# Z's scratch by pairs of classes: two pieces of 90 rows a block, spread over the partitions

## The chip, the cores and the metric

The kernel runs on one NeuronCore of one Trainium2 chip. The metric is the device time of one execution in microseconds; lower is better. PE is the matrix engine (TensorE), DVE the vector engine, ACT the scalar engine, POOL is GpSimd and SP the sync engine. SP and POOL issue all DMAs of this kernel, SP on one queue and POOL on another, and both queues are served by the same 16 DMA engines.

## The reference

The input x has 8 sequences of 5,696 steps with 128 channels; h is one filter of the same length and width. The first half is a causal convolution of x with h by FFTs of double length, the second half a mixing of the lowest 64 frequencies, followed by a dense layer with a ReLU.

```python
def _attn_ref(x, h):
    L = 2 * S
    Xf = np.fft.rfft(x, n=L, axis=1)
    Hf = np.fft.rfft(h, n=L, axis=0)
    return np.fft.irfft(Xf * Hf[None, :, :], n=L, axis=1)[:, :S, :]

def _moe_ref(x, w_r, w_i, w_ch):          # x is the result above
    X = np.fft.rfft(x, axis=1)
    Yr = einsum('bmd,mde->bme', Xr, w_r) - einsum('bmd,mde->bme', Xi, w_i)   # the first 64 modes
    Yi = einsum('bmd,mde->bme', Xr, w_i) + einsum('bmd,mde->bme', Xi, w_r)
    u = x + np.fft.irfft(Y, n=S, axis=1)
    return u + np.maximum(u @ w_ch, 0.0)
```

## The kernel before

A step of the sequence is written as J q + p with J = 64 and q below NQ = 89. The DFT of double length is split into a transform over q, which gives NK = 90 classes, and one over p. The batch is worked in four pairs of sequences (`g_` 0 to 3), and each pair in NT = 23 ticks of KT = 4 classes (the last has two).

In a tick PE forms the spectra of the tick's classes (matmuls of As with M), DVE multiplies them with the filter's (U from Xs and Hs), PE transforms back over p (U with Wc), and ACT writes the result, Z, to a tile of SBUF. A tile of Z has 128 partitions, the real and imaginary part (`ri`) of 64 positions p, and in its free dimension the class, the sequence of the pair and the 128 channels. Z then goes to a scratch in DRAM, `zscr`, one write of 256 KB per tick, issued by SP. PE also uses the Z tile on the spot for the 64 modes (matmuls with G, the accumulator XT).

The output part needs Z the other way round, with the 90 classes and two parts as the contraction. So it reads `zscr` back in 16 blocks, four per pair, each with 16 positions p: 180 rows (class, part) of 8 KB. A block has a room of two tiles, ZTa with rows 0 to 127 and ZTb with rows 128 to 179 in partitions 32 to 83, where partitions 0 to 31 are zero. There are NC = 5 rooms (ZT0 to ZT4), which lie over buffers of the forward part that are dead by then. For each position PE multiplies ZTa with the table S4a (128 rows) and ZTb with S4b (84 rows), into the same accumulator; the term of the 64 modes comes on top (table IB with C). ACT and DVE copy the result to UT, PE multiplies it with the identity and w_ch together (WI), ACT takes the ReLU (R), DVE adds (O), and SP writes the output.

The order is the program's: each operation is recorded with what it reads and writes, and each engine runs its own operations in that order, waiting on semaphores. In the last pair `early` hangs loads for the output part on ticks, all issued by POOL: the identity at tick 0, four parts of the mode weights W at ticks 1, 3, 6 and 8, the table S4b at tick 12, S4a at 16, and at tick 21 blocks 0, 1 and 2 with IB between. Each of those up to tick 16 waits for its tick's U (`pace`). After the last pair POOL issues WI and blocks 3 and 4. Block 0 waits in addition for the Z writes of the last pair's ticks 0 to 14 (`SLACK`). Blocks 5 to 15 are issued by SP, each when the room of the block five ahead of it has been used up, in one queue with the output's writes.

Before it loads a room for the first time, `load_zt` clears partitions 0 to 31 of ZTb with a memset on POOL (L477); the load of that tile follows on the same engine.

While PE waits for the modes' result, it does the Z part of four tiles of block 0 ahead (`u_z(..., alone=True)`); the rest of the work on a tile is in `u_tile`.

Of the kernel before, what the change touches and what calls it, by code (L numbers as in the profile page):

```python
# [4 lines left out]
P = 128  # L5
F16 = mybir.dt.float16
F32 = mybir.dt.float32
U32 = mybir.dt.uint32
# [115 lines left out]
def bass_long_conv_fft__then__afno_spectral_mix_kernel(nc, x, h, moe_w_r, moe_w_i, moe_w_ch, out):  # L124
    B, S, D = x.shape
    M = moe_w_r.shape[0]
    assert D == P and M == 64 and B == 8
    J = 64
    NQ = S // J
# [26 lines left out]
    pos = J * qq[None, :] + pp[:, None]  # L156
    ang = 2.0 * np.pi * kk[:, None, None] * pos[None] / L
    s4 = np.stack([back[:, None, None] * np.cos(ang), -back[:, None, None] * np.sin(ang)], axis=0)
    RB, PB = 2 * NK - P, 32
    rows = s4.transpose(1, 0, 2, 3).reshape(2 * NK, S)  # L160
    s4t = np.zeros((P, 2 * S))
    s4t[:, 0:S] = rows[0:P]
    s4t[PB:PB + RB, S:2 * S] = rows[P:2 * NK]
    tt = np.arange(S)
    am = 2.0 * np.pi * np.outer(tt, np.arange(M)) / S
    modes = np.concatenate([np.cos(am), -np.sin(am)], axis=1)
# [75 lines left out]
    xt = at("XT", B * XTW, F16, a_g + GW * 2 + 2048 * (NZX - NZ))  # L242
    assert GW * 2 + 2048 * (NZX - NZ) + B * XTW * 2 <= HW * 2

    ZB = 16
    NC = 5
    ZP = ZB * 2 * D
# [33 lines left out]
    def pv(bank, off, dims, p0=0, n=P):  # L281
        return bass.AP(ps, p0 * 4096 + bank * 512 + off, [[4096, n]] + [list(d) for d in dims])

    R = Recorder(nc)
    for name, n in (("c", 16), ("x", 26), ("z", 8), ("w", 16), ("t", 10), ("s", 8), ("o", 12), ("p", 16), ("q", 10)):
        R.ring(name, n)

    def bank(i):
        return ("bank", i)
# [18 lines left out]
    def dma(eng, dst, src, ring, reads=(), writes=(), after=()):  # L308
        R.add(eng, lambda h_: h_.dma_start(dst, src), reads, writes, ring=ring, after=after)  # L309

    def mm(o, l, r, st, sp, reads, writes):
        R.add("tensor", lambda h_: h_.matmul(o, l, r, start=st, stop=sp), reads, writes)  # L312
# [3 lines left out]
    def once(key, toks):  # L316
        if key in first:
            return []
        first[key] = 1
        return list(toks)  # L320
# [145 lines left out]
    ZX = [("zs", i, b) for i in range(NZ, NZL) for b in range(2)]  # L466
    zt_old = [(H_ALL, H_ALL), (AST, AST), (H_ALL, H_ALL), (AST, AST), (M_ALL[3:6], G_ALL)]

    def load_zt(i, eng="sync", more=()):
        g_, c_ = divmod(i, J // ZB)  # L470
        for part, (p0, r0, n) in enumerate(((0, 0, P), (PB, P, RB))):
            old = once(("zt", i % NC, part), zt_old[i % NC][part])
            if more:
                old = list(old) + list(more)
            if old and part:
                z32 = zt[i][1][0:PB, :].bitcast(U32)
                R.add("gpsimd", lambda e: e.memset(z32, 0), (), [("zt0", i)], after=old)  # L477
            dma(eng, bass.AP(zt[i % NC][part], p0 * ZP, [[ZP, n], [1, ZP]]),
                bass.AP(zs, (g_ * 2 * NK + r0) * J * 256 + c_ * ZB * 256, [[J * 256, n], [1, ZP]]),
                "q" if eng == "gpsimd" else "t", [("zd", g_, s_) for s_ in range(NT)], [("zt", i % NC, part)], after=old)  # L480

    def load_ib():
        dma("gpsimd", ib_sb[:, :], c_ib.ap(), "p", (), [("ib",)], after=M_ALL[0:2] + pace)

    def load_s4(part):
        n = PB + RB if part else P
        dma("gpsimd", s4_sb[part][0:n, :], bass.AP(c_s4, part * S, [[2 * S, n], [1, S]]), "p", (),
            [("s4", part)], after=pace + (AST if part else M_ALL[1:4]))

    V, A = "vector", "scalar"  # L490
    border = {NT - 1: [(0, 2, V)], NT: [(1, 0, V), (2, 2, A)], NT + 1: [(3, 0, V), (4, 2, A)], NT + 2: [(5, 0, V), (6, 2, V)]}
    early = {0: lambda: load_id(), 1: lambda: load_w(0), 3: lambda: load_w(1), 6: lambda: load_w(2), 8: lambda: load_w(3),
             12: lambda: load_s4(1), 16: lambda: load_s4(0),
             NT - 2: lambda: (load_zt(0, "gpsimd", SLACK), load_ib(), load_zt(1, "gpsimd"), load_zt(2, "gpsimd"))}
    pace = []
    SLACK = [("zd", NP - 1, s_) for s_ in range(NT - NZL)]
# [4 lines left out]
    def load_wi():  # L501
        dma("gpsimd", wi_sb[:, P:2 * P], bass.AP(c_w, 2 * P, [[3 * P, P], [1, P]]), "p", (), [("i16",)], after=M_ALL[5:6])
        dma("gpsimd", wi_sb[:, 0:P], moe_w_ch, "w", (), [("wch",)], after=M_ALL[5:6])
# [33 lines left out]
    def tick(g_, t):  # L537
        if g_ + 1 < NP:
            for i in range(2 * XC):
                if t == XPLACE[g_ > 0][i]:  # L540
                    x_place(i, x_st[i], xtok(i))
        with_h = with_h_at(g_, t)
        if t < NT:
            sl = XSLOT[0] if with_h else XSLOT[(t + (g_ == 0)) % 2]
            for i, k in enumerate(ticks[t]):
                for r in range(2):
                    for b in range(2):
                        col = k * 3 * J + (J if r == 0 else 0) + b * J
                        mm(pv(sl + b, i * D, [[1, D]]),
                           ap(m_sb, MW, J * b, J, col, [[1, P]]),  # L550
                           ap(a_sb, AW, J * b, J, (2 * k + r) * D, [[1, D]]), r == 0, r == 1,
                           AST + mtok(k), [bank(sl + b)])
            products(g_, t, sl)
        if t in border and g_ + 1 < NP:
            for j, sl, e in border[t]:
                a_tile(j, [sl], e)
        if g_ + 1 < NP and t % 2 == 0 and 0 < t <= 4 * XC:
            i = t // 2 - 1
            x_load(g_ + 1, i, x_st[i], xtok(i), [("u", t % NU)] + AST)
        if LC <= t < NT + LC:  # L560
            s_ = t - LC
            n = len(ticks[s_])
            i, zi = s_ % NU, s_ % NZS[g_]
            zb = [turns("z", ZBANK) for b in range(2)]
            for b in range(2):
                for r in range(2):
                    mm(pv(zb[b], 0, [[1, n * D]]), (W1, W2)[r], u_s[i][:, r * 1024 + b * 512:r * 1024 + b * 512 + n * D],
                       r == 0, r == 1, [("u", i), ("wc",)], [bank(zb[b])])
                evac(bass.AP(z_s[zi], b * D, [[1024, P], [2 * D, n], [1, D]]),
                     pv(zb[b], 0, [[D, n], [1, D]]), [bank(zb[b])], [("zs", zi, b)], eng="scalar",  # L570
                     after=once(("zx", zi, b), Z_OLD) if zi >= NZ else ())
            zo = (g_ * NK + KT * s_) * P * 256
            dma("sync", bass.AP(zs, zo, [[256, P], [P * 256, n], [1, 256]]),
                bass.AP(z_s[zi], 0, [[1024, P], [256, n], [1, 256]]), "z",
                [("zs", zi, 0), ("zs", zi, 1)], [("zd", g_, s_)])
        if LM <= t < NT + LM:
            s_ = t - LM
            zi = s_ % NZS[g_]
            if s_ == 0:
                mm(pv(MB, 0, [[1, 2 * P]]), m_sb[ZR:P, 0:P], ap(f1_sb, 2 * NK, ZR, P - ZR, 0, [[0, 2], [1, P]]), True, False, [("f1",)] + mtok(0), [bank(MB)])  # L580
            for i, k in enumerate(ticks[s_]):
                for b in range(2):
                    if k % 2:
                        o, off, n, sl = pv(MB, b * P, [[1, P]]), (k + 1) // 2 * P, P, (k + 1) // 2
                    else:
                        ms, off = even[k]
                        n, sl = 2 * len(ms), 0
                        dims = [[M, 2]] if len(ms) == 1 else [[ms[1] - ms[0], 2], [M, 2]]
                        o = pv(MB, b * P + ms[0], dims)
                    mm(o, z_s[zi][:, i * 256 + b * P:i * 256 + b * P + P], g_sb[:, off:off + n],  # L590
                       False, k == NK - 1 and b == 1, [("g", sl // GP), ("zs", zi, b)], [bank(MB)])
        if with_h:
            filter_tick(t + LH, [2, 3])
# [26 lines left out]
                    dma("gpsimd", dst, src_, ring, (), [tok], after=[("as", j)])  # L620


    load_wi()
    load_zt(3, "gpsimd")
    load_zt(4, "gpsimd")

    LSLOT = [4, 6, 0, 2]
# [4 lines left out]
    def u_z(i, b, half, alone=False):  # L632
        g_, c_ = divmod(i, NCH)
        t = turns("l", LSLOT)
        z = zt[i % NC]
        for hb in range(2):
            if alone:
                mm(pv(t + hb, 0, [[1, 4 * NQ]]), f1_sb[ZR:P, 0:P], ap(f1_sb, 2 * NK, ZR, P - ZR, 0, [[0, 2], [1, 2 * NQ]]),
                   True, False, [("f1",)], [bank(t + hb)])
            else:  # L640
                u_c(i, b, half, t, hb, True)
            for pl in range(4):
                for ri in range(2):
                    pz = half * 8 + hb * 4 + pl
                    so = (c_ * ZB + pz) * NQ
                    n = (P, PB + RB)[ri]
                    mm(pv(t + hb, pl * NQ, [[1, NQ]]), z[ri][0:n, pz * 256 + b * P:pz * 256 + b * P + P], s4_sb[ri][0:n, so:so + NQ],
                       False, not alone and pl == 3 and ri == 1, [("zt", i % NC, ri), ("zt0", i % NC), ("s4", ri)], [bank(t + hb)])
        if alone:
            ahead[(i, b, half)] = t  # L650
        return t
# [149 lines left out]
```

## Time and profile before

Three runs took 405.23, 405.71 and 408.66 us; the median is 405.71. The profiled execution took 409.74 us, of which the profiled span is 407.7 us.

| engine | busy us | share of the span | instructions |
|---|---|---|---|
| PE (matmul) | 376.7 | 92% | 5398 |
| PEld (weight load) | 286.7 | 70% | 5398 |
| DVE | 311.8 | 76% | 341 |
| ACT | 296.4 | 73% | 477 |
| POOL | 81.4 | 20% | 133 |

Over the span the 16 DMA engines moved 105.8 MB, 260 GB/s in the mean, in 86,720 packets. The mean granted clock of PE was 0.977. The four pairs of the forward part end near 272 us, and the output part fills the rest.

The shares are means over stages with different limits, so the windows and the waits say more than this table. A row of the groups gives the line, the engine, what is written from what, the count, the busy time and the mean of one in ns, and the idle time ahead of it with what ended it. Lines 300 to 309 and 312 are helpers (`evac`, `dma`, `mm`), so operations are told apart by their tiles. In this profile ZT0a and ZT0b are the two tiles of a room.

### The profile page before, as it was taken

To read this page: it belongs to the slowest core of one execution; us is meant where nothing else is said; L and a number is where in the kernel's file an instruction comes from. 1 tells how busy PE (TensorE), PEld (TensorE's weight loads), DVE (VectorE), ACT (ScalarE), POOL (GpSimd) and SP (SyncE) were. 2 spreads that over 40 slices of the span, in tenths; PEclk is the share of its full clock that TensorE was granted. 3 is DMA by queue.
4 is the path that set the end of the run, shared out by engine and by line. 5 is a ranking of instruction groups with operands and counts; after the bars stand their busy time and mean duration, and the time that the engine had idled before them with its cause. 6 is when DMAs were issued, how large, how long until landed. Compare 5 with 4: busy or idle time off the path is not lost.

```text
span 407.7 us, 12527 instructions
## 1 busy us (share of the span) xinstructions
PE 376.7 (92%) x5398; PEld 286.7 (70%) x5398; DVE 311.8 (76%) x341; ACT 296.4 (73%) x477; POOL 81.4 (20%) x133
## 2 busy tenths in 40 slices
PE   7979899998999988899989899997978999999994
PEld 7978666656756657656658666665767889888873
DVE  6878789997899997889997888850324677777876
ACT  1458599987978977788878888960434777777775
POOL 8300022210823202723304011039100000000000
PEclk9999999999999999999999999995798999999999
DMA  8997379995989993989985499999998999999869
GB/s 159 194 320 271 101 162 280 274 278 159 138 137 218 251 233 80 141 154 207 245 224 95 48 311 346 285 274 394 417 390 340 314 350 420 406 419 390 347 251 357
DMA packets 86720, 105.81 MB, mean 260 GB/s; under 512 B 22494, under 2 KB 72286, under 8 KB 82846
## 3 DMA queue, kind: packets, MB, share of 16 engines
q1 hardware_dynamic: 62379, 67.73, 48.1%
q0 software_dynamic: 24288, 37.31, 43.0%
q8 instruction: 42, 0.69, 0.7%
q14 instruction: 11, 0.09, 0.1%
HBM read 72.49 MB, written 51.12 MB: 303 GB/s over the span
## 4 chain that ended last, share of the span: by engine, by line
PE 56%; DMA 14%; DVE 11%; ACT 9%; POOL 6%; issue 2%; SPq 0%; DVEq 0%; POOLq 0%
PE ps L312 56%; DVE U L528 5%; DMA ZT4b<-zscr 5%; DVE As L306 5%; DMA Xr<-in_x_dram 4%; ACT As L302 4%; DMA zscr<-Zt 3%; POOL Xr L309 2%; DMA Hs<-Hs 2%; ACT Xs L300 2%; ACT R L735 1%; ACT UT L300 1%; ACT Zt L300 1%; DVE Xin L348 1%; POOL ZT1b L477 0%
## 5 line engine op out<-in xcount | busy, mean ns | idle before, releaser
L528 DVE TENSOR_TENSOR U<-Xs,Hs 128x2048 f16<-128x2048 f16 x70 | 82.7, 1190 | 20.2 <-ACT Xs L300 20.0
L312 PE MATMUL ps<-U,Wc 128*128 128x512 f16 (+1 forms) x368 | 93.6, 377 | 1.9 <-DVE U L528 1.9
L300 ACT CAST Zs<-ps 128x512 f16<-128x512 f32 (+1 forms) x142 | 75.7, 592 | 9.4 <-PE ps L312 9.4
L300 ACT CAST Xs<-ps 128x1024 f16<-128x1024 f32 x70 | 69.4, 996 | 15.6 <-PE ps L312 14.6
L736 DVE TENSOR_TENSOR O<-ps,R 128x512 f32<-128x512 f32 x81 | 52.5, 685 | 20.4 <-ACT R L735 12.0
L735 ACT ACTIVATE R<-ps 128x512 f32<-128x512 f32 x96 | 50.9, 572 | 18.8 <-PE ps L312 18.4
L306 DVE TENSOR_SCALAR As<-ps 128x720 f16<-128x720 f32 x68 | 57.6, 900 | 9.1 <-PE ps L312 8.5
L312 PE MATMUL ps<-As,M 64*128 64x128 f16 x1440 | 55.8, 217 | 5.1 <-ACT Xs L300 2.0
L312 PE MATMUL ps<-F,Xin 128*128 128x180 f16 x512 | 53.5, 249 | 7.0 <-DVE As L306 2.8
L312 PEld LDWEIGHTS ps<-F,Xin 128*128 128x128 f16 x512 | 44.6, 155 | 14.5 <-DVE As L306 4.1
L302 ACT ACTIVATE As<-ps 128x720 f16<-128x720 f32 x60 | 46.3, 785 | 10.6 <-PE ps L312 9.7
L312 PE MATMUL ps<-WI,UT 128*128 128x256 f16 x360 | 52.3, 280 | 0.5 <-DVE O L736 0.4
L312 PEld LDWEIGHTS ps<-As,M 64*128 64x128 f16 x1440 | 40.7, 94 | 15.1 <-DVE U L528 3.2
L312 PEld LDWEIGHTS ps<-U,Wc 128*128 128x128 f16 x368 | 29.1, 98 | 31.6 <-DVE U L528 2.4
L528 DVE TENSOR_TENSOR U<-ps,Hs 128x2048 f16<-128x2048 f32 x22 | 50.2, 2283 | 0.8 <-DMA Hs<-Hs 0.8
L309 POOL DMA_DIRECT2D Xt<-in_x_dram x48 | 25.5, 536 | 109.7 <-PE ps L312 94.7
L300 ACT CAST UT<-ps 128x712 f16<-128x712 f32 x40 | 30.0, 752 | 20.7 <-PE ps L312 19.7
L312 PEld LDWEIGHTS ps<-WI,UT 128*128 128x128 f16 x360 | 39.4, 152 | 4.3 <-issue 1.9
L312 PE MATMUL ps<-IBs,C 128*128 128x356 f16 x128 | 40.6, 327 | 0.6
L312 PEld LDWEIGHTS ps<-G,Zs 128*128 128x128 f16 x556 | 28.1, 96 | 14.9
L304 DVE CAST UT<-ps 128x712 f16<-128x712 f32 x24 | 21.4, 891 | 17.0 <-PE ps L312 17.0
L312 PE MATMUL ps<-G,Zs 128*128 128x128 f16 (+2 forms) x556 | 34.3, 192 | 0.0
(84 smaller groups left out, 497.0 us busy)
## 6 DMA issues: line engine op xcount, KB each, us to landing
out_dram<-O SPq DMA_DIRECT2D x39, 512.0 KB, 8.3
zscr<-Zs SPq DMA_DIRECT2D x68, 256.0 KB, 6.2
Xt<-in_x_dram POOLq DMA_DIRECT2D x24, 320.0 KB, 6.9
zscr<-Zt SPq DMA_DIRECT2D x20, 256.0 KB, 6.9
W<-wscr POOLq DMA_DIRECT2D x4, 1024.0 KB, 8.5
M<-cM POOLq DMA_DIRECT2D x5, 720.0 KB, 20.4
ZT0a<-zscr SPq DMA_DIRECT2D x3, 1024.0 KB, 9.9
Hs<-Hs SPq DMA_DIRECT2D x44, 64.0 KB, 5.9
```

What stands on the lines that cost most here:

```text
L300: R.add(e, lambda h_: h_.copy(dst, src), reads, writes, after=after)
L302: R.add(e, lambda h_: h_.activation(dst, src, COPY, scale=scale), reads, writes, after=after)
L304: R.add(e, lambda h_: h_.tensor_copy(dst, src), reads, writes, after=after)
L306: R.add(e, lambda h_: h_.tensor_scalar_mul(dst, src, scale), reads, writes, after=after)
L309: R.add(eng, lambda h_: h_.dma_start(dst, src), reads, writes, ring=ring, after=after)
L312: R.add("tensor", lambda h_: h_.matmul(o, l, r, start=st, stop=sp), reads, writes)
L348: R.add("vector", lambda e: e.tensor_copy(bass.AP(x_sb, i * XN * XS, [[XW, NQ], [XS, XN], [1, D]]), bass.AP(src, 0, [[XB, NQ], [D, XN], [1 ...
L528: R.add("vector", lambda e: e.tensor_tensor(uv, src, hv, MULT), bk + [("h", t, 0), ("h", t, 1, 0), ("h", t, 1, J)], [("u", i)])
L735: R.add("scalar", lambda e: e.activation(rv, src_r, RELU), bk, [("r", i % NR)], after=once(("r", i % NR), G_ALL + XTT + [("y", 0), ("y", 1 ...
L736: R.add("vector", lambda e: e.tensor_tensor(ov, src_u, rv, ADD), bk + [("r", i % NR)], [key + (h_,)], after=once(key, old))
```

## The change

The scratch is laid out by pairs of classes. A row is now (pair of classes, part) and holds for each position the two classes behind one another: 90 rows of 64 x 512 elements instead of 180 rows of 64 x 256. In a tick's write, one run in DRAM is 1,024 bytes instead of 512.

A room's two tiles no longer hold different rows of a block but its halves: tile 0 the first 8 of the 16 positions, tile 1 the other 8, both with all 90 rows. A row is still 8 KB. `SPREAD` puts the 90 rows on 128 partitions in two pieces: rows 0 to 63 on partitions 0, 2, ..., 126 and rows 64 to 89 on partitions 1, 5, ..., 101. So a block comes in four DMAs instead of two. The other 38 partitions are zero, and each tile is cleared whole before its first load. The clears of rooms 0, 1 and 2 are put into the last pair's ticks 9, 10, 14, 15, 17 and 18; those of rooms 3 and 4 follow the last pair, ahead of the loads of blocks 3 and 4.

The tables S4a and S4b become those of the even and the odd class of a pair. They are loaded in the same two pieces, after a clear of the table; before, the zero rows of S4b came with the load. A matmul reads 128 rows for both classes, and waits only for the pieces of its own half of the block. The rings of semaphores for block loads grow from 10 to 16 (SP) and to 20 (POOL).

```diff
-    RB, PB = 2 * NK - P, 32
-    rows = s4.transpose(1, 0, 2, 3).reshape(2 * NK, S)
...
+    s4t = s4.transpose(1, 0, 2, 3).reshape(NK // 2, 2, 2, S).transpose(0, 2, 1, 3).reshape(NK, 2 * S)
...
+    SPREAD = ((0, J, 0, 2), (J, NK - J, 1, 4))
...
+    def clear_zt(i, h_):
+        z32 = zt[i][h_][:, :].bitcast(U32)
+        R.add("gpsimd", lambda e: e.memset(z32, 0), (), [("zc", i, h_)], after=list(zt_old[i][h_]) + pace)
+
     def load_zt(i, eng="sync", more=()):
         g_, c_ = divmod(i, J // ZB)
-        for part, (p0, r0, n) in enumerate(((0, 0, P), (PB, P, RB))):
-            old = once(("zt", i % NC, part), zt_old[i % NC][part])
...
-            if old and part:
-                z32 = zt[i][1][0:PB, :].bitcast(U32)
-                R.add("gpsimd", lambda e: e.memset(z32, 0), (), [("zt0", i)], after=old)
-            dma(eng, bass.AP(zt[i % NC][part], p0 * ZP, [[ZP, n], [1, ZP]]),
-                bass.AP(zs, (g_ * 2 * NK + r0) * J * 256 + c_ * ZB * 256, [[J * 256, n], [1, ZP]]),
-                "q" if eng == "gpsimd" else "t", [("zd", g_, s_) for s_ in range(NT)], [("zt", i % NC, part)], after=old)
+        n_ = i % NC
+        for h_ in range(2):
+            old = list(once(("zt", n_, h_), zt_old[n_][h_])) + list(more)
+            for part, (r0, n, p0, st) in enumerate(SPREAD):
+                dma(eng, bass.AP(zt[n_][h_], p0 * ZP, [[st * ZP, n], [1, ZP]]),
+                    bass.AP(zs, g_ * NK * P * 256 + r0 * J * 512 + c_ * ZB * 512 + h_ * ZP, [[J * 512, n], [1, ZP]]),
+                    "q" if eng == "gpsimd" else "t", [("zd", g_, s_) for s_ in range(NT)] + [("zc", n_, h_)],
+                    [("zt", n_, h_, part)], after=old)
...
     def load_s4(part):
...
+        s32 = s4_sb[part][:, 0:S].bitcast(U32)
+        R.add("gpsimd", lambda e: e.memset(s32, 0), (), [("s4z", part)], after=old)
+        for h_, (r0, n, p0, st) in enumerate(SPREAD):
+            dma("gpsimd", bass.AP(s4_sb[part], p0 * S, [[st * S, n], [1, S]]), bass.AP(c_s4, (r0 * 2 + part) * S, [[2 * S, n], [1, S]]),
+                "p", [("s4z", part)], [("s4", part, 0, h_)], after=old)
...
+             9: lambda: clear_zt(0, 0),
+             10: lambda: clear_zt(0, 1),
+             14: lambda: clear_zt(1, 0),
+             15: lambda: clear_zt(1, 1),
+             17: lambda: clear_zt(2, 0),
+             18: lambda: clear_zt(2, 1),
...
-            dma("sync", bass.AP(zs, zo, [[256, P], [P * 256, n], [1, 256]]),
-                bass.AP(z_s[zi], 0, [[1024, P], [256, n], [1, 256]]), "z",
+            dma("sync", bass.AP(zs, zo, [[512, P], [P * 512, n // 2], [1, 512]]),
+                bass.AP(z_s[zi], 0, [[1024, P], [512, n // 2], [1, 512]]), "z",
...
+    for h_ in range(2):
+        clear_zt(3, h_)
     load_zt(3, "gpsimd")
+    for h_ in range(2):
+        clear_zt(4, h_)
     load_zt(4, "gpsimd")
...
-                    n = (P, PB + RB)[ri]
-                    mm(pv(t + hb, pl * NQ, [[1, NQ]]), z[ri][0:n, pz * 256 + b * P:pz * 256 + b * P + P], s4_sb[ri][0:n, so:so + NQ],
...
+                    zo = (hb * 4 + pl) * 512 + ri * 256 + b * P
+                    mm(pv(t + hb, pl * NQ, [[1, NQ]]), z[half][:, zo:zo + P], s4_sb[ri][:, so:so + NQ],
```

More of the change, by code (lines that the diff above doesn't have):

```diff
@@ L158, in bass_long_conv_fft__then__afno_spectral_mix_kernel @@
     s4 = np.stack([back[:, None, None] * np.cos(ang), -back[:, None, None] * np.sin(ang)], axis=0)
-    RB, PB = 2 * NK - P, 32
-    rows = s4.transpose(1, 0, 2, 3).reshape(2 * NK, S)
-    s4t = np.zeros((P, 2 * S))
-    s4t[:, 0:S] = rows[0:P]
-    s4t[PB:PB + RB, S:2 * S] = rows[P:2 * NK]
+    s4t = s4.transpose(1, 0, 2, 3).reshape(NK // 2, 2, 2, S).transpose(0, 2, 1, 3).reshape(NK, 2 * S)
     tt = np.arange(S)
@@ L284, in bass_long_conv_fft__then__afno_spectral_mix_kernel @@
     R = Recorder(nc)
-    for name, n in (("c", 16), ("x", 26), ("z", 8), ("w", 16), ("t", 10), ("s", 8), ("o", 12), ("p", 16), ("q", 10)):
+    for name, n in (("c", 16), ("x", 26), ("z", 8), ("w", 16), ("t", 16), ("s", 8), ("o", 12), ("p", 16), ("q", 20)):
         R.ring(name, n)
@@ L467, in bass_long_conv_fft__then__afno_spectral_mix_kernel @@
     zt_old = [(H_ALL, H_ALL), (AST, AST), (H_ALL, H_ALL), (AST, AST), (M_ALL[3:6], G_ALL)]
+    def clear_zt(i, h_):
+        z32 = zt[i][h_][:, :].bitcast(U32)
+        R.add("gpsimd", lambda e: e.memset(z32, 0), (), [("zc", i, h_)], after=list(zt_old[i][h_]) + pace)
     def load_zt(i, eng="sync", more=()):
         g_, c_ = divmod(i, J // ZB)
-        for part, (p0, r0, n) in enumerate(((0, 0, P), (PB, P, RB))):
-            old = once(("zt", i % NC, part), zt_old[i % NC][part])
-            if more:
-                old = list(old) + list(more)
-            if old and part:
-                z32 = zt[i][1][0:PB, :].bitcast(U32)
-                R.add("gpsimd", lambda e: e.memset(z32, 0), (), [("zt0", i)], after=old)
-            dma(eng, bass.AP(zt[i % NC][part], p0 * ZP, [[ZP, n], [1, ZP]]),
-                bass.AP(zs, (g_ * 2 * NK + r0) * J * 256 + c_ * ZB * 256, [[J * 256, n], [1, ZP]]),
-                "q" if eng == "gpsimd" else "t", [("zd", g_, s_) for s_ in range(NT)], [("zt", i % NC, part)], after=old)
+        n_ = i % NC
[6 more added lines that the diff above has]
+                    [("zt", n_, h_, part)], after=old)
     def load_ib():
@@ L485, in load_s4 @@
     def load_s4(part):
-        n = PB + RB if part else P
-        dma("gpsimd", s4_sb[part][0:n, :], bass.AP(c_s4, part * S, [[2 * S, n], [1, S]]), "p", (),
-            [("s4", part)], after=pace + (AST if part else M_ALL[1:4]))
+        old = pace + (AST if part else M_ALL[1:4])
+        s32 = s4_sb[part][:, 0:S].bitcast(U32)
[3 more added lines that the diff above has]
+                "p", [("s4z", part)], [("s4", part, 0, h_)], after=old)
     V, A = "vector", "scalar"
@@ L620, in bass_long_conv_fft__then__afno_spectral_mix_kernel @@
                     dma("gpsimd", dst, src_, ring, (), [tok], after=[("as", j)])
+    pace[:] = []
     load_wi()
+    for h_ in range(2):
+        clear_zt(3, h_)
     load_zt(3, "gpsimd")
+    for h_ in range(2):
+        clear_zt(4, h_)
     load_zt(4, "gpsimd")
@@ L645, in u_z @@
                     so = (c_ * ZB + pz) * NQ
-                    n = (P, PB + RB)[ri]
-                    mm(pv(t + hb, pl * NQ, [[1, NQ]]), z[ri][0:n, pz * 256 + b * P:pz * 256 + b * P + P], s4_sb[ri][0:n, so:so + NQ],
-                       False, not alone and pl == 3 and ri == 1, [("zt", i % NC, ri), ("zt0", i % NC), ("s4", ri)], [bank(t + hb)])
+                    zo = (hb * 4 + pl) * 512 + ri * 256 + b * P
+                    mm(pv(t + hb, pl * NQ, [[1, NQ]]), z[half][:, zo:zo + P], s4_sb[ri][:, so:so + NQ],
+                       False, not alone and pl == 3 and ri == 1,
+                       [("zc", i % NC, half)] + [("zt", i % NC, half, v_) for v_ in range(2)] + [("s4", ri, 0, 0), ("s4", ri, 0, 1), ("s4z", ri)], [bank(t + hb)])
         if alone:
```

## The prediction

> **What bounds the kernel now.** I read the page first (span, slices, queues), then the waits of PE, the chain of waits, the windows around the border between the last pair's forward part and the output part, and last the trace's records of single DMA packets.
>
> ```profile
> span 407.7 us, 12527 instructions
> ...
> q1 hardware_dynamic: 62379, 67.73, 48.1%
> q0 software_dynamic: 24288, 37.31, 43.0%
> ```
>
> The two queues kept the 16 DMA engines busy 91% of the span. The windows (us; busy PE, PEld, DVE, ACT, POOL; clock; DMA share; GB/s) show where that matters:
>
> ```profile
> 230.00:240.00 10.00, 8.69 (x124) 5.02 (x125) 8.79 (x6) 7.95 (x13) 1.08 (x2) 1.00 0.60 172
> ...
> 242.00:271.00 29.00, 29.00 (x432) 18.18 (x429) 23.86 (x16) 26.10 (x44) 2.14 (x4) 1.00 1.03 313
> 271.00:291.00 20.00, 17.03 (x253) 12.69 (x251) 2.46 (x5) 4.18 (x9) 15.58 (x18) 0.66 1.00 368
> 291.00:307.00 16.00, 12.18 (x218) 10.35 (x215) 4.34 (x5) 6.02 (x8) 0.00 (x0) 0.99 0.99 400
> 307.00:404.00 97.00, 94.51 (x1222) 82.08 (x1222) 71.98 (x114) 70.39 (x126) 0.00 (x0) 0.98 0.92 362
> ```
>
> Up to 271 PE is full, so DMA time there costs nothing by itself. From 242 to 307 DMA never rests, and from 271 to 307 PE does: PE waits for blocks of Z. After 307 PE is the bound again (94.5 of 97 us), with DMA close behind at 0.92, 89 us of 97. PE's waits in 270 to 320 (total, times, longest) name the blocks:
>
> ```profile
> PE ps L312 <- DMA ZT4b<-zscr: 2.4, 1, 2.4
> PE ps L312 <- DMA ZT0b<-zscr: 2.4, 1, 2.4
> PE ps L312 <- DMA ZT3b<-zscr: 0.7, 1, 0.7
> PE ps L312 <- DMA ZT4a<-zscr: 0.7, 1, 0.7
> ```
>
> The chain (start, us, what) runs through POOL's issues at the border:
>
> ```profile
> 260.02 10.88 DMA zscr<-Zt
> ...
> 271.42 0.53 POOL ZT0a L309
> 271.95 1.81 POOL ZT0b L477
> 273.76 0.46 POOL ZT0b L309
> ...
> 286.47 20.44 DMA ZT4b<-zscr
> 306.91 0.04 issue
> ```
>
> The 20.44 us after the last issue are a queue, not latency. The packet records give medians of 27 ns for 512 bytes, 46 for 1,024, 309 for 8,192 and 427 for 11,392 (the times on SP's queue add to 3,138 us, the page's 48.1% of 16 x 407.7). Of POOL's queue from 271.4: five blocks, 5 x 180 x 309 / 16 = 17.4 us; the IB table, 128 x 427 / 16 = 3.4; beside them the last eight ticks' Z, 7.5 x 512 x 27 / 16 = 6.5. Alone it would end at 298.7. SP starts on blocks 5 to 8 at 290.8 and takes half: the end is 2 x 298.7 - 290.8 = 306.6; measured 306.9. So one us saved ahead of 291 brings block 4 two us forward, and one lost sends it two back.
>
> **The parts that cost nothing.** PE does the same number of matmuls, and 84 rows cost what 128 do:
>
> ```profile
> L312 PE MATMUL ps<-S4b,ZT2b 84*128 84x89 f16 x96 | 11.0, 204 | 0.0
> L312 PE MATMUL ps<-S4a,ZT2a 128*128 128x89 f16 x96 | 11.0, 203 | 0.0
> ```
>
> POOL gets ten clears of 128 x 2048 words, at 1.82 us from the 32 x 2048 row of L477 if partitions run side by side, and two of 2848 words for the tables, 2.53 each by length. Eight of these twelve (16.0 us) go into the last pair, where POOL is busy 2.1 us of 29. Each waits for its tick's U and stands ahead of the next tick's, 1.85 us later; with the second table's clear and two issues at tick 16 they pile up, and POOL is free at 260.9 + 2.53 + 1.07 + 2 x 1.82 = 268.1. S4a is issued 3 us later (264 for 260.9). It took 9.4 to land, so 273.4 against its first use at 278.2; that margin covers it. At the border POOL issues 20 pieces, IB and two WI at 0.53 and four clears: 12.2 + 7.3 = 19.5 us where it was 15.6. From 268.1 that ends at 287.6 (before: 287.0), and the queue ahead of block 4 holds work beyond that, so nothing waits. If the cover went, up to 3.9 us would show. SP issues 22 more loads at about 0.42 us, 9 us; it waits 63 us for DVE's O, which hides them, and the out_dram writes queued behind move by under 1 us each.
>
> **What it saves.** Packets of Z double from 512 to 1,024 bytes. From 242 to 307 the records have 10,495 of 512: 10,495 x 27 / 16 = 17.7 us; half as many of 46 make 15.1: minus 2.6. Earlier pairs save as much per tick, but under a full PE: zero. Also PE starts block 0's first half when two of four pieces are in, so the 2.4 us wait for ZT0b can go.
>
> **What it may cost.** Block loads carry the same bytes in the same 8 KB rows, but no longer 128 and 52 rows on neighbouring partitions: 64 rows on every second partition, 26 on every fourth. No row of the trace shows such a transfer. The lower bound is 309 ns a packet, factor f = 1. The upper one comes from the nearest transfer of another shape, S4b with 84 rows:
>
> ```profile
> S4a<-cS POOLq DMA_DIRECT2D x1, 1424.0 KB, 9.4
> ...
> S4b<-cS POOLq DMA_DIRECT2D x1, 934.5 KB, 8.5
> ```
>
> S4b moved two thirds of S4a's bytes in nine tenths of its time. Its packets have a median of 718 ns where IB's 128 rows have 427, and in the middle, with little other traffic, 731, while 15 of the 84 ran at 427 or a little more: most of its engines held each other up, f = 1.7. The 64-row Hs copies show the same, 68 ns for 46 in the burst at 50.2 (1.5). In both, the rows crowd the lower half of the partitions, which the new pieces avoid; but four rows of an engine now reach over eight partitions, so two engines may still meet. Between 1 and 1.7 neither is nearer: I take the middle, f = 1.35.
>
> The Trainium skill's "SBUF — State Buffer", section Door 1: The DMA port swizzle, says a DMA's rate goes by how many of 16 ports its partitions reach, and that partitions 0 to 63 reach eight. By it the crowding explains S4b, the trace agrees (84 rows were slow), and the new pieces, which reach all 16 evenly, would have f = 1; that is the first rival below. Against the change speaks "DMA: Bandwidth & Descriptors", section Latency and other measured facts: row pitches of large powers of two slow HBM copies, 207 GB/s at 512 KiB. The rows' pitch goes from 32 to 64 KB; no run here shows what that does, and at half rate f would be 2.
>
> **The sum.** End of POOL's queue alone: 298.7 - 2.6 + tables + 17.4 (f - 1). The tables before: 128 x 427 + 84 x 716 (S4b's mean), 7.2 us; after: 180 x 427 x f / 16 = 4.8 f. SP starts when block 0 is used up, 290.8 before; with ZT0's wait gone 288.4.
> - f = 1: 298.7 - 2.6 - 2.4 = 293.7; block 4 at 2 x 293.7 - 288.4 = 299.0, before PE asks (303.6 less the 2.4). PE gains all its waits: 2.4 + 0.7 + 0.7 + 2.4 = 6.2, minus 6.
> - f = 1.35: 298.7 - 2.6 - 0.7 + 6.1 = 301.5; block 0 lands about when PE is ready, so 288.5; block 4 at 314.5, 7.6 later than 306.9.
> - f = 1.6: 307.0, with 290 for SP: 324, plus 17.
> After that PE's 97 us run on. DMA's 89 us contain seven to eight blocks of 3.5: at 1.35 they add 9 us, 98, a us over; at 1.6 it is 16, some 8 over, partly drained while PE waited. PE also falls to a clock of 0.50 when it waits (the 278 to 287 window), another us. My value is 7.6 + 1 + 1, plus 9.
>
> The profiled execution took 409.74 us, 2.0 around a span of 407.7; the median shown is 405.7, 1% below. The difference is carried over to the median: 405.7 + 9 is about 415 (418.7 beside the profiled one).
>
> **The rivals.**
> 1. Faster: the spread rows do not meet. For it: the 128- and 52-row loads run at 309 ns from 284 to 307, and all partitions are used evenly. Against it: S4b and Hs. It gives 405.7 - 6 = 399.7 and decides from f below 1.09, where block 4 lands 4 us earlier.
> 2. Cancelled out: f from 1.09 to 1.27. The packets saved and the packets lengthened are about equal; f = 1.18 puts block 4 at 306.9, so 405.
> 3. Slower by POOL, not by DMA: the clears hold DVE up in the last pair. DVE's slack there is about 0.27 us a tick; 16.0 us of clears over ten ticks could cost up to 13, so 418. Against it: the Y cast at 275.6 ran inside a POOL memset and took 0.69, as the Hs casts of that shape (0.683). That the table clears make the tables late is part of this one.
>
> **How the numbers follow.** Forecast (f above 1.27): 0.43, own range 410 to 424; rival 3: 0.04; rival 1: 0.35; rival 2: 0.18. A measurement of this kernel tells about 1% (4 us) from no change. Slower by over 1% is 0.43 + 0.04 = 0.47, within 0.18, faster 0.35. For 8 in 10 the range reaches from just below rival 1, 399, to f = 1.6, 424.
>
> **What would show it.** Right: zscr writes as 1,024-byte packets; in 271 to 307 the DMA share stays at 1.0 but GB/s falls below the 368 and 400 of now; block loads take over 12 us to land on SP's queue; PE's longest wait is for a ZT4 piece, beyond 310. Wrong: 8 KB rows stay near 309 ns and the PE waits at the border vanish (rival 1). If DVE's U rows grow beyond 1.22 us at ticks 9 to 18, rival 3.

## The result and the profile after

The changed kernel took 427.77 us (median of four runs, 424.88 to 430.26) against 405.47 for the kernel before (four runs); the ratio is 1.050, 95% interval 1.042 to 1.057. The direction was forecast, the size was not: 415 had been said, and 424 was the end of the range. The profiled execution took 426.73 us around a span of 424.8, 17.1 us more than the span before. In later comparisons the kernel before had medians of 407.5 to 409.6 in 17 to 28 runs each, so a few of the 22 us probably belong to the small number of its first runs. Below, kernels are compared by their ratios to the runs of the kernel before that were made beside them.

The page shows the change at work: the packets fell from 86,720 to 64,160, as twice 512 bytes became once 1,024.

```profile
span 424.8 us, 12597 instructions
...
DMA packets 64160, 105.46 MB, mean 248 GB/s; under 512 B 23005, under 2 KB 49757, under 8 KB 60317
```

The same windows as before (PE, PEld, DVE, ACT and POOL busy; clock; DMA share; GB/s):

```profile
242.00:271.00 29.00, 29.00 (x440) 18.25 (x438) 23.96 (x16) 26.11 (x44) 18.78 (x14) 1.00 0.96 314
271.00:291.00 20.00, 19.68 (x285) 14.53 (x284) 4.34 (x7) 6.20 (x13) 19.03 (x27) 0.74 1.00 332
291.00:307.00 16.00, 9.54 (x126) 7.56 (x123) 2.70 (x3) 3.38 (x5) 0.00 (x0) 0.79 1.01 299
307.00:330.00 23.00, 16.46 (x211) 14.10 (x211) 6.70 (x10) 8.20 (x13) 0.00 (x0) 0.78 0.82 254
```

Up to 271 PE stays full. From 271 to 307 the DMA engines are as busy as before, and carry less: 332 and 299 GB/s for 368 and 400. That is what slow packets look like: a full share with a low rate. PE waits for blocks 2, 3 and 4 where it waited for 0, 3 and 4 (its waits in 265 to 330; total, times, longest):

```profile
PE ps L309 <- DMA ZT2b<-zscr: 4.4, 1, 4.4
PE ps L309 <- DMA ZT3a<-zscr: 3.4, 1, 3.4
PE ps L309 <- DMA ZT3b<-zscr: 3.4, 1, 3.4
PE ps L309 <- DMA ZT4b<-zscr: 1.1, 1, 1.1
PE ps L309 <- DMA ZT2a<-zscr: 0.8, 1, 0.8
```

In sum 13.1 us for 6.2. In the chain the last piece of block 4 takes 31.87 us behind its issue where it took 20.44, and PE goes on at 322.2 instead of 306.9:

```profile
271.82 1.05 POOL ZT0a L306 x2
...
290.32 31.87 DMA ZT4b<-zscr
322.24 10.90 PE ps L309 x161
```

So 15.3 of the 17.1 us have gone by then. (The profile of the kernel before caught an execution in which PE waited for block 4. In two later kernels with the same border, below, block 4 landed at 303.7 and 303.9; beside these the changed kernel is 18 us late.) The records of single DMA packets from 271 up to that point add to 49.7 us of all 16 engines where they were 35.7. POOL's blocks have 900 packets of 423 ns in the mean instead of 331 (23.8 us for 18.6). SP's blocks got in 618 packets of 439 instead of 437 of 322 (17.0 for 8.8). Over the whole output part the 2,880 packets of the 16 blocks took 410 ns in the mean instead of 335.

### The profile page after: what moved, and what is told of

Read it like the earlier page. It is cut to its first block, busy times and chain, and to the rows that moved or that the text cites. A ratio compares the mean times of both kernels' runs of the same rounds, so it can differ in the third digit from the quotient of the medians.

```text
span 424.8 us, 12597 instructions
## 1 busy us (share of the span) xinstructions
PE 381.7 (90%) x5398; PEld 288.9 (68%) x5398; DVE 312.1 (73%) x341; ACT 296.6 (70%) x477; POOL 101.3 (24%) x152
## 2 busy tenths in 40 slices
DMA packets 64160, 105.46 MB, mean 248 GB/s; under 512 B 23005, under 2 KB 49757, under 8 KB 60317
## 4 chain that ended last, share of the span: by engine, by line
PE 48%; DMA 19%; DVE 14%; ACT 8%; POOL 7%; issue 4%; DVEq 0%; POOLq 0%
PE ps L309 48%; DMA ZT4b<-zscr 8%; DVE U L536 7%; DVE As L303 5%; DMA Xr<-in_x_dram 4%; DMA out_dram<-Os 4%; ACT As L299 3%; DMA Xt<-in_x_dram 3%; ACT Xs L297 2%; POOL Xr L306 2%; ACT R L749 1%; ACT UT L297 1%; DVE Xin L345 1%; DVE Hs L301 1%; POOL ZT4a L468 0%
## 5 line engine op out<-in xcount | busy, mean ns | idle before, releaser
L309 PE MATMUL ps<-F,Xin 128*128 128x180 f16 x512 | 54.8, 254 | 7.0 <-DVE As L303 2.9
L309 PEld LDWEIGHTS ps<-F,Xin 128*128 128x128 f16 x512 | 45.7, 155 | 14.7 <-DVE As L303 4.5
L299 ACT ACTIVATE As<-ps 128x720 f16<-128x720 f32 x60 | 46.3, 786 | 11.8 <-PE ps L309 10.9
L309 PE MATMUL ps<-IBs,C 128*128 128x356 f16 x128 | 42.8, 344 | 4.0 <-DVE Os L750 3.2
```

The lines of the kernel that those rows point to most:

```text
L299: R.add(e, lambda h_: h_.activation(dst, src, COPY, scale=scale), reads, writes, after=after)
```

## The experiments

**The loads by themselves.** Eight stages, each loading eight blocks of 8 KB rows with nothing else running.

```diff
+PHASES = [("A", "aligned32", "sync"), ("B", "aligned64", "sync"), ("C", "spread64", "sync"), ("D", "spread32", "sync"),
+          ("E", "contig64", "sync"), ("F", "sixty64", "sync"), ("G", "aligned64", "gpsimd"), ("H", "spread64", "gpsimd")]
...
+                for s, dst, src in ops:
+                    h_.dma_start(dst, src).then_inc(sems[s], 16)
+                for s, v in waits:
+                    h_.wait_ge(sems[s], v)
```

> Leaves out the whole computation: it only loads blocks, eight per stage, one stage after another, from the input x in place of the scratch, with rows of 8 KB. Stages by name of the tiles: RA rows 128 and 52 as before the change, row pitch 32 KB; RB the same rows at a pitch of 64 KB; RC the pieces of the change (64 rows on every second, 26 on every fourth partition), pitch 64 KB; RD the same pieces at 32 KB; RE the 90 rows on partitions 0 to 89, pitch 64 KB; RF 60 rows on partitions 32 to 91, 16 on every second from 0, 14 on every second from 92, pitch 64 KB; all these from SP. RG and RH are RB and RC from POOL. A stage moves 11.8 MB. Theory 1 (placing: the DMA engines get in each other's way at the partitions): RA, RB and RG run at 309 ns a packet, some 28 us a stage and over 400 GB/s; RC, RD and RH at about 415 ns, 37 to 40 us, 300 GB/s; RE at 440 ns or more; RF at 309 ns for two packets in three. Theory 2 (pitch of 64 KB): RA and RD are fast, RB, RC, RE, RF slow alike. Theory 3 (number of pieces, four for two): C, D, E alike and F slower still, A and B fast.

The windows cut at the first issue of each stage A to H (length; DVE and POOL busy; clock; DMA share; GB/s):

```profile
0.74:32.94 32.20, 1.76 (x1) 0.00 (x0) 1.00 0.89 366
32.94:64.78 31.84, 0.00 (x0) 0.00 (x0) 1.00 0.89 371
64.78:109.61 44.83, 0.00 (x0) 0.00 (x0) 1.00 0.89 263
109.61:154.26 44.65, 0.00 (x0) 0.00 (x0) 1.00 0.89 264
154.26:211.31 57.05, 0.00 (x0) 0.00 (x0) 1.00 0.92 207
211.31:257.52 46.21, 0.00 (x0) 0.00 (x0) 1.00 0.88 256
257.52:290.62 33.10, 0.00 (x0) 8.51 (x17) 1.00 0.87 356
290.62:330.90 40.28, 0.00 (x0) 16.62 (x32) 1.00 0.91 293
```

A and B are alike, C and D are alike: the pitch of 64 KB does nothing, the pieces and their placing everything. The mean packet is 316 and 315 ns in A and B, 437 in C and D, 575 in E, 448 in F, 318 in G and 402 in H. The pieces of the change cost a factor of 1.38 from SP and 1.26 from POOL. Theory 1 stands, except at F, where it expected two packets in three at 309 ns: 9% were below 320. E and C have the same number of pieces and differ by 12 us, and six pieces in F cost 1.4 us more than four in C, so the number of pieces alone isn't it either.

The port rule of the Trainium skill ("SBUF — State Buffer", Door 1: The DMA port swizzle) agrees with E against C, since partitions 0 to 63 reach only half the ports. It does not cover C against A: by the page's table C's 90 rows reach all 16 ports with five or six rows each, and C is 12.6 us slower. The Trainium skill's row on the pitch of rows ("DMA: Bandwidth & Descriptors", Latency and other measured facts), which the prediction quoted with 207 GB/s at 512 KiB, has 214 as the full rate, so 207 was hardly slow. At 64 KB there is no loss here: B took 31.84 us, A 32.20.

**The 90 rows on partitions 0 to 89.**

```diff
-    SPREAD = ((0, J, 0, 2), (J, NK - J, 1, 4))
+    SPREAD = ((0, J, 0, 1), (J, NK - J, J, 1))
```

> The changed kernel with its 90 rows on partitions 0 to 89 (64 and 26 rows, no gaps). Theory 1 (placing): 64 rows crowd the lower half of the partitions as S4b's 84 did; packets of 500 ns or more, so 1.6 for 1.35 and slower than the changed kernel by 5 to 12 us, 432 to 440. Theory 2 (pitch): as the changed kernel, 427.

It took 453.83 us, ratio 1.115 (1.107 to 1.123). Slower than the changed kernel, by more than the expected 432 to 440: alone, these loads have a factor of 1.82, not 1.6. So the spread pieces are better than 90 neighbouring rows, and the gap to the old placing stays.

**60, 16 and 14 rows.**

```diff
-    SPREAD = ((0, J, 0, 2), (J, NK - J, 1, 4))
+    SPREAD = ((0, 60, 32, 1), (60, 16, 0, 2), (76, 14, 92, 2))
```

> The changed kernel with its 90 rows in three pieces: 60 on partitions 32 to 91, where each of 15 engines has four neighbouring partitions to itself, 16 on every second from 0 and 14 on every second from 92. Six DMAs a block. Theory 1 (placing): two packets in three at 309 ns, the factor falls from 1.35 to 1.1 to 1.2, 402 to 412. Theory 2 (pitch): as the changed kernel, 427. Theory 3 (number of pieces): slower than the changed kernel.

432.62 us, ratio 1.060 (1.055 to 1.065): a miss, no faster than the changed kernel. Stage F says the same. My reading, argued and not tried: a small piece that lands where another engine is writing slows both, so 30 of 90 rows out of place disturb 60.

**The border, taken out of the kernel before.** SP's first load waits for block 4.

```diff
-                "q" if eng == "gpsimd" else "t", [("zd", g_, s_) for s_ in range(NT)], [("zt", i % NC, part)], after=old)
+                "q" if eng == "gpsimd" else "t", [("zd", g_, s_) for s_ in range(NT)] + [("zt", 4, v_) for v_ in range(2) if i == NC],
+                [("zt", i % NC, part)], after=old)
```

> The kernel before, with SP's first block load (block 5) held until block 4 has landed. By the term 'SP takes half' of the prediction block 4 then lands near 299 instead of 307, PE's waits for ZT3b, ZT4a and ZT4b (0.7 + 0.7 + 2.4) go, and the kernel gets 3 to 4 us faster, 402. Rival: PE meets the same wait at block 5 or 6, no gain.

411.29 us, ratio 1.008 (1.004 to 1.011): a miss, although the waits it was to remove are gone; PE's waits for DMA shrank to 1.0 us for ZT0b. But it is not shown that the hold removed them. In two kernels below that leave the border as it was, the late copies and the kernel before with half the output, PE does not wait for block 4 either; of the second, all of PE's waits behind 268 are:

```profile
PE ps L312 <- DMA ZT0b<-zscr: 3.4, 1, 3.4
PE ps L312 <- DVE O L736: 0.4, 1, 0.4
```

What the hold itself did shows in the queue. From POOL's first block load to the landing of block 4's last piece it took 28.7 us; in those two it took 33.0 and 33.4, in the profile of before 35.5. But in this execution POOL's first load went out at 273.7, 2.3 us later than in that of before. Block 4 was in use at 304.8 instead of 306.9, and the rest took 105.2 us instead of 100.8. There the chain runs through the output's writes, and DVE waits for them.

```profile
359.92 0.70 DVE Os L737
360.64 15.32 DMA out_dram<-Os
```

**The same hold in the changed kernel.** The edit is that of the last, for four pieces.

> The changed kernel with SP's first block load held until all of block 4 has landed. Theory B (border; the prediction's model: what counts is when block 4 lands, after that PE is the bound): block 4 lands some 10 us earlier and the kernel gains 6 to 8 us against the changed one, about 420. Theory D (the output part as a whole goes by the time of its DMAs, whatever their order): as the changed kernel, 426 to 431.

423.67 us, ratio 1.041 (1.033 to 1.050), 0.9 points better than the changed kernel, which the two intervals alone do not separate; the traces do. Block 4's last piece is in use at 304.6 instead of 322.2, so taking SP's packets (17.0 us) out of the way brought it forward by about as much (POOL's first load also went out 2.0 us earlier here). PE starts the block at 303.05 instead of 319.6, 16 us earlier, and only 4.7 of the span arrive at the end. DVE's waits show where the rest went:

```profile
DVE Os L751 <- DMA out_dram<-Os: 9.9, 4, 3.2
DVE O L751 <- DMA out_dram<-O: 4.6, 3, 3.9
```

In the changed kernel these two were 3.6 and 2.1. Neither theory is enough: the border counts, and behind it the DMA engines are a limit of their own.

**More DMA at the border, and more behind it.** A copy of 128 rows of 4 KB, within DRAM, ahead of blocks 0 to 4 in one kernel (shown) and of blocks 9 to 15 in the other (`if i >= 9`).

```diff
+        if i < NC:
+            dma(eng, bass.AP(spare, i * P * 2048, [[2048, P], [1, 2048]]),
+                bass.AP(zs, g_ * 2 * NK * J * 256 + c_ * ZB * 256, [[J * 256, P], [1, 2048]]), ...
```

> The kernel before with one copy more ahead of each of blocks 0 to 4: 128 rows of 4 KB from the scratch to a spare place in DRAM, some 160 ns a packet, so 1.3 us of all 16 DMA engines each, 6.4 in all, at the border. Theory B: doubled by SP's share, plus 10 to 13 us. Theory D: plus 6.4, once.

> The kernel before with the same copy ahead of each of blocks 9 to 15, all behind the border: 7 times 1.3, 8.9 us of DMA. Theory B (PE is the bound behind block 4, DMA has 8 us of room): plus 0 to 2 us. Theory D: plus 7 to 9 us.

The first took 420.10 us, ratio 1.032 (1.024 to 1.039), some 13 us; PE begins block 4 at 315.26 instead of 304.32, 10.9 us later. The copies' records add to 7.3 us (182 ns a packet, not the 160 expected). Block 4's last piece lands at 316.6, 9.7 us later than in the profile of before and 12.8 later than in the two kernels in which PE did not wait for it. So a us ahead of block 4 costs 1.3 to 1.8 there: more than once, not quite twice. The second took 415.60, ratio 1.020 (1.012 to 1.029), some 8 us for 8.9. So each theory was right at its own place: beside the 97 us of PE behind block 4 there is no room for 9 us more of DMA.

**Two limits.** From this came theory L: the end is set by the later of two things, block 4's arrival plus some 100 us of PE, and the whole DMA time of the output part. Half of each output row is left out in the next three.

```diff
-            dst = bass.AP(out.tensor, ..., [[NW * D, P], [1, w_]])
-            src = ob[:, 0:w_]
+            dst = bass.AP(out.tensor, ..., [[NW * D, P], [1, w_ // 2]])
+            src = ob[:, 0:w_ // 2]
```

> The changed kernel, writing only the first half of each output row (2,048 of 4,096 bytes; the other half is left out), so some 28 us less DMA in the output part. Theory L (two limits: block 4 in, plus some 100 us of PE; and the output part's DMA time end to end, plus some 10 us; the later one counts): block 4 still lands near 322, so 420 to 428, little gain. Theory D (DMA time alone): 15 us or more faster than the changed kernel, about 410.

> The same with SP's first block load held until block 4 has landed: half of each output row is left out, the slow block loads stay. Theory L: both limits are lifted (block 4 near 303, DMA 28 us shorter), so as the kernel before, 404 to 411, though the blocks load as slowly as in the changed kernel. Theory B (border alone): as the held changed kernel with full output, 420 to 424.

> The kernel before, writing only half of each output row. Theory L: block 4 at 307 and PE's 100 us stay, 0 to 4 us faster. Theory D: 15 us or more faster.

The changed kernel with half the output: 420.21 us, ratio 1.033 (1.027 to 1.038). The same with the hold: 409.74, ratio 1.006 (1.002 to 1.010). The kernel before with half the output: 405.85, ratio 0.996 (0.992 to 0.999). All three as theory L has it; theory D fails at the first and third, theory B at the second. With both limits lifted the slow loads, still 393 ns a packet, cost 0.6% against the kernel before, and 1.0% against the kernel before with half the output. Of the change's five points about 3.5 stand without the DMA limit (420.21 against 405.85); the rest is the DMA limit.

The records from 271 to the end add up as follows. (271 is a fixed cut. In all but the last kernel POOL's first block load goes out between 269.8 and 273.7. The last column is theory L's reading.)

| kernel | DMA us | span less 271 | engines idle | limit |
|---|---|---|---|---|
| before | 127.9 | 136.7 | 8.8 | both |
| changed | 142.4 | 153.8 | 11.4 | both |
| before, held | 129.4 | 139.0 | 9.6 | DMA |
| changed, held | 138.4 | 149.1 | 10.7 | DMA |
| extra copies late | 135.2 | 143.5 | 8.3 | DMA |
| extra copies early | 132.8 | 147.8 | 15.0 | block 4 |
| changed, half the output | 117.3 | 148.0 | 30.7 | block 4 |
| before, half the output | 104.4 | 130.9 | 26.5 | PE |
| changed, held, half the output | 111.3 | 135.2 | 23.9 | PE |
| W earlier, S4b of 52 rows (next) | 127.5 | 133.9 | 6.4 | both |
| the same and block 0 early (last) | 125.4 | 131.3 | 5.9 | both |

Where DMA is a limit, the engines idle 6 to 11 us; where it isn't, 15 and more.

**Less DMA ahead of the border.** W at earlier ticks, S4b as 52 rows.

```diff
-    early = {0: lambda: load_id(), 1: lambda: load_w(0), 3: lambda: load_w(1), 6: lambda: load_w(2), 8: lambda: load_w(3),
+    early = {0: lambda: (load_w(0), load_w(1), load_id()), 1: lambda: load_w(2), 2: lambda: load_w(3),
...
+        if part:
+            s32 = s4_sb[1][0:PB, 0:S].bitcast(U32)
+            R.add("gpsimd", lambda e: e.memset(s32, 0), (), [("s4z",)], after=old)
+        p0, n = (PB, RB) if part else (0, P)
```

> The kernel before with two savings of DMA time ahead of the border: the mode weights W are loaded at ticks 0, 0, 1 and 2 of the last pair instead of 1, 3, 6 and 8 (the DMA engines idle a third of 230 to 240), and S4b comes as 52 rows on partitions 32 to 83 with its zero rows cleared by POOL instead of as 84 rows from partition 0 (3.8 us of packets, 1.4 by the 427 ns of other rows). Theory D: 3 to 4 us plus 2.4 us less DMA behind 242, so 4 to 6 us faster. Theory B: the same or more at the border, up to the 6 us that PE waits there. Rival: no gain, the forward part is held by the heavier traffic at its start.

408.79 us, ratio 1.001 (0.997 to 1.005): nothing, as the rival had it. S4b's 52 packets took 2.4 us, not 1.4. The DMA time it freed ahead of 271 stayed empty: 0.69 of the engines from 255 to 260, where it was 0.99. From 271 on there was as much to do as before (127.5 us).

**And block 0 loaded into that gap.**

```diff
-             12: lambda: load_s4(1), 16: lambda: load_s4(0),
-             NT - 2: lambda: (load_zt(0, "gpsimd", SLACK), load_ib(), load_zt(1, "gpsimd"), load_zt(2, "gpsimd"))}
+             12: lambda: load_s4(1), 9: lambda: load_zt(0, "gpsimd"), 16: lambda: load_s4(0),
+             NT - 2: lambda: (load_ib(), load_zt(1, "gpsimd"), load_zt(2, "gpsimd"))}
```

> The kernel before with W loaded at ticks 0, 0, 1 and 2, S4b as 52 rows, and block 0 loaded at tick 9 of the last pair instead of tick 21, into the DMA time that the first two free (0.69 of 255 to 260 was used with these two alone). So one block, 3.5 us of DMA, leaves the output part, and PE's wait for ZT0b (2.4 to 3.1) goes. Theory L: both limits come forward by 3 us, 403 to 406 beside 409. Theory B: the same or less. Rival: no gain, as with the two savings alone (ratio 1.001).

403.47 us, ratio 0.990 (0.987 to 0.994): 1% faster than the kernel before, as theory L expected. PE no longer waits for any block at the border, and 125.4 us of DMA are left behind 271. From 271 to 307 PE is busy 35.78 us of 36, where it was 29.21, and 32.40 in the kernel before with half the output, which did not wait for block 4 (the three in the order before, before with half the output, this kernel):

```profile
271.00:307.00 36.00, 29.21 (x466) 23.04 (x464) 6.81 (x9) 10.19 (x17) 15.58 (x18) 0.81 0.99 382
271.00:307.00 36.00, 32.40 (x514) 26.61 (x513) 8.40 (x11) 11.74 (x20) 14.90 (x17) 0.81 1.01 385
271.00:307.00 36.00, 35.78 (x566) 28.86 (x565) 10.92 (x16) 15.63 (x28) 12.76 (x15) 0.86 1.02 386
```

## Why the prediction was right in kind and wrong in size

The step that failed is block 4's arrival: the sum put it at 314.5 and it came at 322.2. POOL's queue was credited with 3.3 us of savings that lie ahead of its start and moved nothing, and SP's share of the engines grew with that delay. Beside it the DMA time of the output part was taken for a us over, and it was a second limit as late as the first.

- **What bounds the kernel** was read rightly up to 307: PE waits for blocks, and DMA never rests. "After 307 PE is the bound again, with DMA close behind" was read as room of 8 us. The late copies show that there is none: 8.9 us of packets cost some 8.
- **One us at the border is two at block 4**: right in kind; in the early copies it was 1.3 to 1.8. In the changed kernel the rule gives 2 x 305.2 - 286.7 = 323.7 with the measured terms below, for 322.2.
- **The free parts** were free. U's rows did not grow beside the clears (the longest from 242 on in the last pair is 1.23 us for Xs, as before), so rival 3 is out:

```profile
L528 DVE TENSOR_TENSOR U<-Xs,Hs 128x2048 f16<-128x2048 f16 x70 | 82.7, 1190 | 20.2 <-ACT Xs L300 20.0
L536 DVE TENSOR_TENSOR U<-Xs,Hs 128x2048 f16<-128x2048 f16 x70 | 82.7, 1189 | 21.8 <-ACT Xs L297 21.6
```

The upper row is that of before. A clear took 1.82 us on 128 partitions as on 32, one of the tables 2.48 for 2.53. But POOL being free at 268.1 (in fact 269.6) did not start block 0 then. Its load waits for the filter's readers up to tick 21, whose U ended near 271.8:

```profile
271.82 1.05 POOL L306 DMA_DIRECT2D ZT0a<-zscr  x2 [2.18 <-DVE U L536]
```

- **What it saves, minus 2.6 and minus 0.7**: the first failed term. The end of POOL's queue was counted from its start at 271.4, and most of what was saved lies before. Z's packets did shrink, 20.5 to 17.1 us behind 225. Since nothing could be issued earlier, the saving turned into idle engines (share 1.03 to 0.96 from 242 to 271); Z's part behind 271 was 3.9 us for 4.0. POOL's queue alone would have ended at 322.2 - 17.0 = 305.2, where 301.5 was said: 3.7 us, of which these two terms are 3.3 and the later start (271.8) 0.4. That the same count gave 298.7 for the kernel before, where it was 306.9 - 8.8 = 298.1, was partly luck: Z's packets behind 271 were 4.0 us instead of 6.5, the blocks 18.6 instead of 17.4. Only the wait for ZT0b went, as said.
- **What it costs, f = 1.35**: right on its own base of 309 ns: 1.39 up to block 4's landing, 1.33 over all 16 blocks. Beside the means of the kernel before, which were above 309, it was 1.28 on POOL's packets and 1.36 on SP's up to there, and 1.22 over all blocks; alone it was 1.38 and 1.26. Rivals 1 and 2 asked for f below 1.27 on the prediction's base and fell with it. That it was right is in part luck, as the middle of two bounds. One of the two witnesses for the upper bound was also misread: half of the Hs copies write to partitions 64 to 127, so the Hs copies as a whole do not crowd the lower half.
- **SP's half share**: the second failed term, by the first and not by its rule. It was put at 314.5 - 301.5 = 13 us and was 17.0. It stretches with each us that POOL's queue is late, and SP began at 286.7, not 288.5: with the halves of a block in separate tiles its first load goes when half of block 0 is used up. Together with the first, block 4 came at 322.2 instead of 314.5, plus 15.3 and not plus 7.6. The hold, which takes this share out, has block 4 in use at 304.6.
- **"After that PE's 97 us run on"**: the third. In the profiled pair this part grew by 1.8 us, about as said. But the limit behind it was missed: 16 blocks at f = 1.35 are 19.5 us more DMA by the prediction's own terms, in a part whose engines idle 9 us; only the seven to eight blocks behind 307 were counted. The records grew by 14.5 us, 13.5 of them in the blocks, whose packets had taken 335 ns and not 309 in the kernel before. With the engines idle 11.4 us instead of 8.8 that is the 17.1 of the spans. The two limits lay so close together in the kernel before that the change ran into both, and that is why neither the hold nor the halved output brings it back alone.
- **The carry to the median**: the profiled execution of before was 4 us above its median, so plus 17 in the spans is plus 22 between the medians. In the later runs of the kernel before the medians were 2 to 4 us higher, so the first few were low.
- **The signs**: two of the four did not come. The 64-row loads on SP's queue took 9.6 to 13.2 us (medians by tile), mostly under 12. PE's longest wait was not for block 4: it paid for the slow queue piece by piece, 4.4 us for ZT2b, 3.4 each for ZT3a and ZT3b, 1.1 for ZT4b.

## What to carry to other kernels

Where DMA is full over a stretch, total its time over the whole stretch first, and only then look at the one wait that ends last; a gain on either limit is lost if the other stands beside it. A saving shortens a queue only if it falls behind the queue's start. Time saved on a full queue is worth something only if later work can be issued into it. Before rows are moved to other partitions, time the bare loads: the same bytes in the same rows took 1.4 times as long.

## What the runs showed of the hardware

- By themselves, loads of 8 KB rows run at 309 ns a packet (median; mean 316) with 128 rows on all partitions and 52 rows on partitions 32 to 83. With 64 rows on every second and 26 on every fourth partition they average 437 ns from SP and 402 from POOL, with 90 rows on partitions 0 to 89 575, and with 60, 16 and 14 rows 448. The first and the last of these three lie on partitions 0 to 126 and 0 to 118, the 90 neighbouring rows on 0 to 89. Why the wide spread is not enough is open: the records do not name the DMA engine.
- A read pitch of 64 KB costs nothing against 32 KB (31.84 and 32.20 us a stage).
- Packets of 1,024 bytes take 46 ns and of 512 bytes 27, so doubling the run saves 15% of the time, not half.
